# A second MLP in blocks of 512 tokens: first product wider, its weights read again per block

## The chip, the cores and the metric

The kernel runs on one core of a Trainium2 chip. The metric is the device time of one execution in microseconds (us), as the median of several runs.

## The reference

Attention with two kinds of window feeds two MLPs in a row; x is 2304 tokens by 512, both MLPs have 2048 hidden columns. The change touches the second MLP alone:

```python
def _moe2_ref(x, w_in, w_out):
    h = x @ w_in                           # 2304 x 2048
    relu6 = np.clip(h + 3.0, 0.0, 6.0)
    g = h * relu6 / 6.0
    return (g @ w_out).astype(np.float32)  # 2304 x 512
```

## The kernel before, in words

Products are made in three passes of fp32r matmuls (`PASSES`, L624): every operand is split into a high part (a rounded copy, `copy`, L244) and a low part (the rest, `sub`, L247), and high·high, high·low and low·high are summed in PSUM.

**First MLP** (`tile1`, L637): six blocks of 384 tokens, 16 tiles each. A tile is 12 matmuls of the first product (`h`, 384 columns, L629), the activation on ScalarE and VectorE in a buffer of the ring `e` (three buffers; taken by `neg`, L646, free after the split `lo`, L675), and 12 matmuls of the second product (`yp`, L684). The result goes to DRAM as `x2d`.

**Second MLP** (`tile2`, L834): nine blocks `b` of 256 tokens (`N2`), eight tiles `j` each, 72 in all. A tile has two parts.

- The first product `hq`, here called F: two times 12 matmuls of 256 columns (`gemm1`, L626) into one PSUM bank of 512 columns. The weights `w1_i_0`, 16 tiles of 512 KB in the ring `w0`, are loaded once (L792) while the last block of the first MLP frees their buffers, and then stay. One `relu` on ScalarE (L849) and one `mul` on VectorE (L852) over 512 columns make g.
- The second product `m`, here called S: a seven-product (Strassen) scheme, 21 matmuls of 256 columns (L899) in four PSUM banks (`PRODS`, L831). Before it VectorE makes five sums of parts of g (`gf`, L865 to L871), ScalarE rounds (`ga`, `gz`, L245) and VectorE subtracts (`ga`, `gz`, L248). Four of its weight parts stay (`w1_i_1`, L796); the three others, `wx`, 768 KB a tile, stay for even `j` and are read again in each block for odd `j` (L823): 40 loads.

The tokens of a block (`load_x2`, L748) come as four loads of 128 KB from `x2d` (L761) into buffers of the ring `y` (first block) or `e`, then a rounded copy on ScalarE and a subtraction (VectorE or GpSimd in the first block, GpSimd alone later). After the last tile of a block, `y2_out` (L949) adds the seven products up: two copies on ScalarE (L976), eight adds on VectorE (L981), four stores.

The order on every engine is made by a planner (`Plan.run`, L106). Each job has a key (its due time), the engines that can do it with a modelled cost, and what it needs; a ring gives a buffer when its last users have been planned. At each step the job that can start first is taken, the lower key at a tie, and instructions are emitted in that order. On the chip each engine works in that fixed order and waits at each instruction for what it needs. All transfers are issued from SyncE (SP), in order too.

Of the kernel before, what the change touches and what calls it, by code (L numbers as in the profile page):

```python
# [19 lines left out]
P = 128  # L20
# [32 lines left out]
    FULL=("0p0", "0d0", "0d1", "1p0", "1d0", "1d1"),  # L53
    BIAS=0.6,
# [134 lines left out]
def tile_window_attention_two_mlps(  # L189
# [50 lines left out]
    SIZES = dict(w0=KF, w1=KF, raw=3, stg=3, x=4, e=3, y=4, ghl=4, gz=2, wx0=KP // 2, wx1=2, s=2, st=4, a=2, h=2)  # L240
# [22 lines left out]

    SL2 = 5.4

    def at2(b, j):
        return TB[NB1] + SL2 * (b * KP + j)

# [476 lines left out]

    x2, x2_ready, x2_users = {}, {}, {}

    def load_x2(b):  # L748
        key = at2(b - 1, 1) if b else at2(0, 0) - 20
        xu = x2_users[b] = [], []  # L750
        blocks = range(b * N2 // T1, ((b + 1) * N2 - 1) // T1 + 1)
        first = None
        after = tiles2[b - 1, 1][0] if b else tiles[NB1 - 1, 5][0]
        x2_ready[b] = []
        for c in range(KD):
            r, yu = {}, []
            ring = "e" if b else "y"

            def load(e, c=c, r=r):
                r["y"] = take(gp, ring, [P, N2], F32, f"y2_{b}_{c}")  # L760
                nc.sync.dma_start(out=r["y"], in_=x2d[:, c, b * N2:(b + 1) * N2])  # L761

            def hi(e, c=c, r=r):
                if c == 0:
                    x2[b] = [take(xp, "x", [P, 2, 2, N2], F32R, f"x2_{b}_{z}") for z in range(2)]
                copy(e, x2[b][c // 2][:, 0, c % 2], r["y"])

            def lo(e, c=c, r=r):
                z = x2[b][c // 2]
                sub(e, z[:, 1, c % 2], r["y"], z[:, 0, c % 2].bitcast(F32))  # L770

            k = key + c * SL2 * 0.8
            l = job(k, load, {"S": 0.42}, [after, *(x2_done[n, c] for n in blocks)], 0.4, [(RINGS[ring], yu)])
            h = job(
                k + 2, hi, {"A": C["A"](N2)}, [l, first], 0,
                [(RINGS["x"], xu[0]), (RINGS["x"], xu[1])] if c == 0 else (),
            )
            first = first or h
            lj = job(k + 2.1, lo, {"P": C["P"](N2), "D": C["D"](N2)} if not b else {"P": C["P"](N2)}, [h])
            yu += [l, h, lj]  # L780
            xu[c // 2].extend([h, lj])
            x2_ready[b].append(lj)

    def load_w2(i):
        key = at1(NB1 - 1, i) + CFG["LAG"]
        j, k = divmod(i, 2)
        u0 = w_users[1, i, 0] = []
        u1 = w_users[1, i, 1] = []

        def l0(e):  # L790
            w = w_t[1, i, 0] = take(wpool, "w0", [P, 2, DM], F32R, f"w1_{i}_0")
            nc.sync.dma_start(out=w.bitcast(F32), in_=w2d[0][:, i])  # L792

        def l1(e):
# [5 lines left out]
        w2j[i, 0] = job(key, l0, {"S": 0.42}, [last[0], *(w2_done[0, i, c] for c in range(2))], 1.3, [(RINGS["w0"], u0)])  # L800
        w2j[i, 1] = job(key + 0.1, l1, {"S": 0.42}, [last[1], *(w2_done[1, j, 2 * k + c] for c in range(2))], 1.3, [(RINGS["w1"], u1)])
# [3 lines left out]
    def phase(e):  # L805

        p1.close()
        p2["wx"] = ctx.enter_context(tc.tile_pool(name="wx", bufs=KP // 2))
        p2["gt"] = ctx.enter_context(tc.tile_pool(name="gt", bufs=2))

    def load_wx(b, j):

        if j % 2 == 0 and b:
            return wx_j[b - 1, j]
        ring = f"wx{j % 2}"
        u = w_users[2, b, j] = []
        key = at2(b, j) - 11 if b or j % 2 and j > 3 else at1(NB1 - 1, j) + 4

        def load(e):
            if "wx" not in p2:  # L820
                phase(e)
            w = w_t[2, j] = take(p2["wx"], ring, [P, 3, 2, EH], F32R, f"wx{j}_{b}")
            nc.sync.dma_start(out=w.bitcast(F32), in_=w2d[1][:, j, 4:7])  # L823

        return job(key, load, {"S": 0.42}, [*prep_last, *att_users], 2.0, [(RINGS[ring], u)])

    wx_j = {}
    m_tags = deque(["a", "a", "h", "y0", "y1", "y2", "y3"])
# [3 lines left out]
    m_users, tiles2 = {}, {}  # L832

    def tile2(b, j):  # L834


        key = at2(b, j)
        r = {}

        def g1(k):  # L840
            def fn(e):
                if k == 0:
                    r["h"] = ps.tile([P, 2, N2], F32, tag="h", name=f"hq{b}_{j}", bufs=SIZES["h"])
                gemm1(w_t[1, 2 * j + k, 0], x2[b], r["h"][:, k])
            return fn

        def relu(e):
            r["e"] = take(gp, "ghl", [P, 2, N2], F32, f"g{b}_{j}")
            nc.scalar.activation(out=r["e"], in_=r["h"], func=AF.Relu, bias=3.0)  # L849

        def mul(e):
            nc.vector.scalar_tensor_tensor(  # L852
                out=r["e"], in0=r["e"], scalar=6.0, in1=r["h"], op0=ALU.min, op1=ALU.mult
            )


        parts = lambda: r["e"].rearrange("p k (t c) -> p (k t) c", c=P)

        def sums(n):
            def fn(e):  # L860
                if n == 0:
                    r["f"] = take(gp, "ghl", [P, 5, P], F32, f"gf{b}_{j}")
# [18 lines left out]
        def z_hi(e):  # L881
            r["z"] = take(p2["gt"], "gz", [P, 2, 5, P], F32R, f"gz{b}_{j}")
            copy(e, r["z"][:, 0], r["f"])
# [4 lines left out]
        def g2(e):  # L888
            ms = ys.setdefault(("m", b), {})
            for n, bank_ in enumerate(PRODS):  # L890
                if j == 0:
                    y = ps.tile([P, 2, EH], F32, tag=tags[n], name=f"m{b}_{n}", bufs=SIZES.get(tags[n], 1))
                    for z, (k, _, _) in enumerate(bank_):
                        ms[k] = y[:, z]
                for z, (k, ka, kb) in enumerate(bank_):
                    w = w_t[1, 2 * j + kb // 2, 1][:, kb % 2] if kb < 4 else w_t[2, j][:, kb - 4]
                    for s, (a, c) in enumerate(PASSES):
                        g = r["a"][:, a, ka] if ka < 2 else r["z"][:, a, ka - 2]
                        nc.tensor.matmul(  # L899
                            ms[k], g, w[:, c, :], start=(j == 0 and z == 0 and s == 0),  # L900
                            stop=(j == KP - 1 and z == len(bank_) - 1 and s == 2),
                        )

        t = 3 * KD * C["R"](N2)
        hu, eu, fu, au, zu = [], [], [], [], []
        prev = tiles2.get((b, j - 1) if j else (b - 1, KP - 1))
        need = [w2j[2 * j, 0], prev[1] if prev else None]
        if j == 0:
            need += x2_ready[b]
        j1 = job(key, g1(0), {"T": t}, need, 0, [(RINGS["h"], hu)])  # L910
        j2 = job(key + 0.5, g1(1), {"T": t}, [j1, w2j[2 * j + 1, 0]])
        for z in range(2):
            x2_users[b][z].extend([j1, j2])
        w_users[1, 2 * j, 0].append(j1)
        w_users[1, 2 * j + 1, 0].append(j2)
        j3 = job(key + 0.6, relu, {"A": C["A"](2 * N2)}, [j2], 0, [(RINGS["ghl"], eu)])
        j4 = job(key + 0.7, mul, {"D": C["D"](2 * N2)}, [j3])
        j4.sbuf = False
        hu += [j2, j3, j4]
        s = [  # L920
            job(key + 0.8, sums(0), {"D": C["D"](N2)}, [j4], 0, [(RINGS["ghl"], fu)]),
        ]
        s += [job(key + 0.81 + 0.01 * n, sums(n), {"D": C["D"](P if n == 1 else N2)}, [s[0]]) for n in (1, 2)]
        j5 = job(key + 0.9, a_hi, {"A": C["A"](N2)}, [j4], 0, [(RINGS["ghl"], au)])
        j6 = job(key + 0.95, z_hi, {"A": C["A"](5 * P)}, s, 0, [(RINGS["gz"], zu)])
        j7 = job(key + 1.0, a_lo, {"D": C["D"](N2)}, [j5])
        j8 = job(key + 1.1, z_lo, {"D": C["D"](5 * P)}, [j6])
        eu += [j4, *s, j5, j7]
        fu += [*s, j6, j8]
        need = [j7, j8, w2j[2 * j, 1], w2j[2 * j + 1, 1], wx_j[b, j], prev[2] if prev else None]  # L930
        takes = []
        if j == 0:
            tags = []
            m_users[b] = [[] for _ in PRODS]
            for n in range(len(PRODS)):
                tags.append(m_tags[0])
                takes.append((RINGS[m_tags[0]], m_users[b][n]))
                m_tags.rotate(-1)
# [10 lines left out]
    def y2_out(b, key, last):  # L949
# [3 lines left out]
        for u in mu:  # L953
            u.append(last)
# [195 lines left out]
```

## Time and profile before

| | us |
|---|---|
| median of three runs (894.13 to 894.49) | 894.15 |
| profiled execution | 894.27 |
| its span, first to last instruction | 892.3 |

The profiled execution lies 0.12 us above the median, and 1.97 us of it lie outside the span. Times in rows count from the start of the span; mean durations are in ns. PE is TensorE, PEld its weight loads, DVE VectorE, ACT ScalarE, POOL GpSimd, SP the queue of SyncE. A matmul's own duration is longer than the distance to the next one, since they are pipelined: the rate is read from starts.

### The profile page before, as it was taken

How to read it: one execution, taken by the hardware profiler on the slowest of the kernel's cores; microseconds unless marked ns; L12 is line 12 of the kernel's file. 1: busy time of each engine (PE TensorE's matmuls, PEld its weight loads, DVE VectorE, ACT ScalarE, POOL GpSimd, SP SyncE). 2: the span in 40 equal slices, each digit the busy share in tenths (PEclk: the TensorE clock that was granted, in tenths of full speed). 3: DMA queues.
4: the chain of work that ended last, by engine and by line, in shares of the span. 5: the costliest groups of instructions: out<-in, count | busy, mean ns of one | idle time of the engine just before them, and what ended most of it. 6: DMA issues, size and time to landing. Idle time of an engine off the chain costs nothing.

```text
span 892.3 us, 17756 instructions
## 1 busy us (share of the span) xinstructions
PE 865.9 (97%) x6972; PEld 845.0 (95%) x6972; DVE 573.8 (64%) x1244; ACT 428.2 (48%) x1086; POOL 146.0 (16%) x156
## 2 busy tenths in 40 slices
PE   4699999999999999999999999999999999999997
PEld 4599999999999999999999999999999999999997
DVE  6998997878778764543333556565656565756565
ACT  4887865766766763443232333343433343333332
POOL 2655631422323310000000101010101010101000
PEclk9899999999999999999999999999999999999999
DMA  9956548787687862102988523232323232323231
GB/s 347 366 212 245 183 138 276 254 291 250 233 281 266 282 205 86 69 25 78 328 274 255 187 71 119 72 118 72 119 72 119 72 119 72 118 71 119 72 100 54
DMA packets 60627, 149.27 MB, mean 167 GB/s; under 512 B 6272, under 2 KB 28288, under 8 KB 60544
## 3 DMA queue, kind: packets, MB, share of 16 engines
q1 hardware_dynamic: 60544, 148.14, 49.1%
q8 instruction: 55, 0.90, 0.4%
q14 instruction: 28, 0.23, 0.1%
HBM read 115.61 MB, written 32.51 MB: 166 GB/s over the span
## 4 chain that ended last, share of the span: by engine, by line
PE 87%; DVE 5%; DMA 5%; ACT 2%; issue 1%; SPq 0%; POOL 0%; DVEq 0%; ACTq 0%
PE yp L684 21%; PE h L629 21%; PE hq L629 20%; PE m L899 18%; DMA y<-x2d 2%; DVE raw L304 1%; DMA raw<-in_w_in_dram 1%; DMA kTd<-in_kd_dram 1%; DMA w2do<-stg 1%; DVE gz L248 1%; ACT gz L245 0%; DMA vd<-in_vd_dram 0%; DVE gf L871 0%; ACT raw L293 0%; DVE gf L869 0%
## 5 line engine op out<-in xcount | busy, mean ns | idle before, releaser
L629 PE MATMUL hq<-x,w 128*128 128x256 f32 x1728 | 219.2, 283 | 0.0
L684 PE MATMUL yp<-ghl,w 128*128 128x384 f32 x1152 | 218.9, 338 | 0.0
L629 PEld LDWEIGHTS hq<-x,w 128*128 128x128 f32 x1728 | 212.7, 192 | 0.0
L684 PEld LDWEIGHTS yp<-ghl,w 128*128 128x128 f32 x1152 | 199.3, 188 | 1.5
L852 DVE SCALAR_TENSOR_TENSOR g<-g,hq 128x512 f32<-128x512 f32 x72 | 49.4, 686 | 115.5 <-ACT g L849 115.5
L629 PE MATMUL h<-xp,w 128*128 128x384 f32 x576 | 119.3, 341 | 0.0
L629 PE MATMUL h<-xd,w 128*128 128x384 f32 x576 | 115.9, 335 | 1.4 <-DVE xd L561 1.3
L849 ACT ACTIVATE g<-hq 128x512 f32<-128x512 f32 x72 | 43.0, 597 | 144.3 <-PE hq L629 144.1
L648 ACT ACTIVATE e<-h 128x384 f32<-128x384 f32 x96 | 47.2, 492 | 128.6 <-PE h L629 128.3
L629 PEld LDWEIGHTS h<-xd,w 128*128 128x128 f32 x576 | 101.3, 188 | 2.0 <-DVE xd L561 1.5
L629 PEld LDWEIGHTS h<-xp,w 128*128 128x128 f32 x576 | 99.2, 188 | 1.4
L662 DVE SCALAR_TENSOR_TENSOR e<-e,h 128x384 f32<-128x384 f32 x96 | 52.6, 549 | 66.5 <-ACT e L651 66.5
L899 PE MATMUL m<-w,gz 128*128 128x256 f32 x648 | 91.2, 284 | 1.8 <-DVE gz L248 1.7
L248 POOL TENSOR_TENSOR x<-y,x 128x256 fp32r<-128x256 f32 x32 | 25.2, 801 | 401.8 <-ACT x L245 401.8
L899 PEld LDWEIGHTS m<-w,gz 128*128 128x128 f32 x648 | 83.2, 192 | 3.1 <-DVE gz L248 2.7
L248 DVE TENSOR_TENSOR gz<-gf,gz 128x640 fp32r<-128x640 f32 x72 | 59.8, 830 | 35.7 <-ACT gz L245 34.6
L245 ACT CAST gz<-gf 128x640 fp32r<-128x640 f32 x72 | 52.4, 728 | 53.5 <-DVE gf L871 53.5
L899 PE MATMUL m<-wx,gz 128*128 128x256 f32 x432 | 63.6, 283 | 0.0
L248 DVE TENSOR_TENSOR ghl<-e,ghl 128x384 fp32r<-128x384 f32 x90 | 54.5, 606 | 5.5 <-ACT ghl L245 4.1
L899 PEld LDWEIGHTS m<-wx,gz 128*128 128x128 f32 x432 | 57.0, 192 | 0.0
L304 DVE SCALAR_TENSOR_TENSOR raw<-raw 128x512 int32<-128x512 int32 x64 | 51.3, 806 | 5.9 <-ACT raw L293 4.0
L248 POOL TENSOR_TENSOR w<-raw,w 128x512 fp32r<-128x512 f32 x32 | 46.3, 1457 | 35.8 <-DVE w L245 15.6
(438 smaller groups left out, 1044.0 us busy)
## 6 DMA issues: line engine op xcount, KB each, us to landing
wx<-w2do SPq DMA_DIRECT2D x40, 768.0 KB, 4.3
raw<-in_w_in_dram SPq DMA_DIRECT2D x32, 512.0 KB, 6.1
raw<-in_w_out_dram SPq DMA_DIRECT2D x32, 512.0 KB, 6.3
w2do<-stg SPq DMA_DIRECT2D x56, 256.0 KB, 2.5
w2di<-stg SPq DMA_DIRECT2D x32, 256.0 KB, 4.3
w<-w2di SPq DMA_DIRECT2D x16, 512.0 KB, 4.5
w<-w2do SPq DMA_DIRECT2D x16, 512.0 KB, 4.5
qd<-in_qd_dram SPq DMA_DIRECT2D x12, 512.0 KB, 4.4
```

The source lines that it names most:

```text
L245: (nc.scalar.copy if e == "A" else nc.vector.tensor_copy)(out=out, in_=in_)
L248: ENG[e].tensor_tensor(out=out, in0=in0, in1=in1, op=ALU.subtract)
L304: nc.vector.scalar_tensor_tensor(out=hi(), in0=hi(), scalar=3, in1=lo(), op0=ALU.logical_shift_left, op1=ALU.bitwise_or)
L629: nc.tensor.matmul(h, w[:, a, c * P:(c + 1) * P], x[c // 2][:, b, c % 2, :], start=(c == 0 and s == 0), stop=(c == KD - 1 and s == 2),)
L648: nc.scalar.activation(out=r["e"], in_=r["h"], func=AF.Relu, scale=-1.0)
L662: nc.vector.scalar_tensor_tensor(out=r["e"], in0=r["e"], scalar=-1.0, in1=r["h"], op0=ALU.add, op1=ALU.max)
L684: nc.tensor.matmul(ys[b, n], w[:, a, n * P:(n + 1) * P], g[:, c, :], start=(i == 0 and s == 0), stop=(i == KF - 1 and s == 2),)
L849: nc.scalar.activation(out=r["e"], in_=r["h"], func=AF.Relu, bias=3.0)
L852: nc.vector.scalar_tensor_tensor(out=r["e"], in0=r["e"], scalar=6.0, in1=r["h"], op0=ALU.min, op1=ALU.mult)
L899: nc.tensor.matmul(ms[k], g, w[:, c, :], start=(j == 0 and z == 0 and s == 0), stop=(j == KP - 1 and z == len(bank_) - 1 and s == 2),)
```

## The change: what it does

- The first product takes 512 tokens at a time (`N1`): four blocks `c` of 512 and a last one of 256, eight tiles `j` each, 40 in all. A tile is again two times 12 matmuls, now of 512 columns, each dozen in its own PSUM bank (ring `h`, two banks, no longer shared with `m`).
- g is made per half of 256 tokens: `relu` and `mul` over 256 columns, 144 of each instead of 72 over 512. It stays in a new ring `g` of twelve buffers until the second product of that half.
- The second product keeps its 256 tokens. It runs at least `S2` = 5 first-product tiles behind; its sums and splits are due `LEAD2` = 6 us ahead. It is issued in two jobs, of 12 matmuls (banks 0 and 1) and 9 (banks 2 and 3). `gz` moves to the ring `x` (four buffers instead of two), `gf` to a ring of its own (two).
- The ring `w0` now holds the block's tokens (four buffers a block) beside the first product's weights, which are read again for each block: 80 loads of 512 KB instead of 16, each due after the load eight places before it has been used. `wx` is read for every tile: 72 loads instead of 40, in a ring of three, each after the second product three before it.
- All token loads go through the ring `e`, also those of the first block, and their subtractions may go to VectorE or GpSimd.

```diff
-    SIZES = dict(w0=KF, w1=KF, raw=3, stg=3, x=4, e=3, y=4, ghl=4, gz=2, wx0=KP // 2, wx1=2, s=2, st=4, a=2, h=2)
+    SIZES = dict(w0=KF, w1=KF, raw=3, stg=3, x=4, e=3, y=4, ghl=4, wx=3, g=12, f=2, s=2, st=4, a=2, h=2)
...
+    N1 = 2 * N2
+    NB3 = -(-NT // N1)
+    NH = lambda c: min(NT - c * N1, N1) // N2
+    def times2():
+        t = TB[NB1]
+        todo = [(2 * c + h, j) for c in range(NB3) for h in range(NH(c)) for j in range(KP)]
+        for n in range(NB3 * KP):
+            c, j = divmod(n, KP)
+            first2[c, j] = t
+            t += 6 * KD * C["R"](NH(c) * N2)
+            while todo and len(second2) < 2 * (n + 1 - CFG["S2"]) and todo[0][0] // 2 * KP + todo[0][1] < n:
+                second2[todo.pop(0)] = t
+                t += 21 * C["R"](EH)
...
+    def load_x2(c):
+        for k in range(KD):
+            for h in range(NH(c)):
+                key = first2[c - 1, k + 2] + h if c else first2[0, 0] - 20 + 4 * k
+                after = tiles[NB1 - 1, k + 12 * c][0] if c < 2 else tiles2[c - 2, KP - 1]
...
+                    r["y"] = take(gp, "e", [P, N2], F32, f"y2_{c}_{k}_{h}")
...
+                        x2[c, k] = take(wpool, "w0", [P, 2, NH(c) * N2], F32R, f"x2_{c}_{k}")
...
+                after0 = tiles2[c - 1, 0] if c else tiles[NB1 - 1, 3][0]
...
+                lj = job(key + 2.1, lo, {"P": C["P"](N2), "D": C["D"](N2)}, [x])
...
+    def load_w0(c, i):
+        def load(e):
+            w = w_t[3, c, i] = take(wpool, "w0", [P, 2, DM], F32R, f"w1_{c}_{i}_0")
+            nc.sync.dma_start(out=w.bitcast(F32), in_=w2d[0][:, i])
+        n = len(seq2)
+        seq2.append((c, i))
+        last = tiles[NB1 - 1, 4 + n][0] if n < KP else tiles2[seq2[n - KP][0], seq2[n - KP][1] // 2]
+        key = first2[c, i // 2] - 16
...
-        if j % 2 == 0 and b:
-            return wx_j[b - 1, j]
...
+        after = done2[divmod(n - 3, KP)] if n > 2 else start2
+        wx_j[b, j] = job(second2[b, j] - 11, load, {"S": 0.42}, [after, start2], 2.0, [(RINGS["wx"], u)])
...
-    m_tags = deque(["a", "a", "h", "y0", "y1", "y2", "y3"])
+    m_tags = deque(["a", "a", "y0", "y1", "y2", "y3"])
...
+    def gemm2nd(c, j):
+        for k in range(2):
+            def g1(e, r=r, k=k):
+                r["h"] = ps.tile([P, n], F32, tag="h", name=f"hq{c}_{j}_{k}", bufs=SIZES["h"])
+                w = w_t[3, c, 2 * j + k]
+                for d in range(KD):
+                    for s, (a, z) in enumerate(PASSES):
+                        nc.tensor.matmul(r["h"], w[:, a, d * P:(d + 1) * P], x2[c, d][:, z, :],
+                            start=(d == 0 and s == 0), stop=(d == KD - 1 and s == 2))
...
+                def relu(e, r=r, b=b, h=h, k=k):
+                    nc.scalar.activation(out=g_t[b, j][:, k], in_=r["h"][:, h * N2:(h + 1) * N2], func=AF.Relu, bias=3.0)
...
-        j9 = job(key + SL2 + 3.0, g2, {"T": 21 * C["R"](EH)}, need, 0, takes)
+        for n, (banks, size) in enumerate((((0, 1), 12), ((2, 3), 9))):
+            prev = job(
+                key + n * 12 * C["R"](EH), g2(banks), {"T": size * C["R"](EH)}, [*need, prev], 0,
+                [(RINGS[m_tag[b, k]], m_users[b][k]) for k in banks] if j == 0 else (),
+            )
```

## Rows read from the trace of the kernel before

**Rows 1.** The page: busy time by engine; the granted clock in 40 slices.
```profile
PE 865.9 (97%) x6972; PEld 845.0 (95%) x6972; DVE 573.8 (64%) x1244; ACT 428.2 (48%) x1086; POOL 146.0 (16%) x156
...
PEclk9899999999999999999999999999999999999999
```

**Rows 2.** Busy time by stage: the second MLP, and the last 10 us.
```profile
core 0: us, PE busy (x) PEld busy (x) DVE busy (x) ACT busy (x) POOL busy (x), PEclk, DMA share, GB/s
490.70:892.30 401.60, 395.35 (x3266) 393.58 (x3264) 236.74 (x507) 141.72 (x269) 25.16 (x32) 1.00 0.31 97
881.90:892.30 10.40, 5.60 (x43) 5.00 (x41) 5.55 (x14) 2.39 (x5) 0.00 (x0) 0.95 0.15 51
```

**Rows 3.** Timeline, TensorE: starts of S (its first three matmuls) in the second MLP.
```profile
500.75 0.52 PE L899 MATMUL m<-wx,ga 128*128 128x256 f32 x3
...
593.21 0.52 PE L899 MATMUL m<-wx,ga 128*128 128x256 f32 x3
599.21 0.52 PE L899 MATMUL m<-wx,ga 128*128 128x256 f32 x3
...
881.80 0.52 PE L899 MATMUL m<-wx,ga 128*128 128x256 f32 x3
```

**Rows 4.** The chain that ended last, 584 to 600 us: start us, us, what.
```profile
586.49 5.49 DMA y<-x2d
...
593.48 1.15 DVE gz L248
...
594.67 1.82 PE m L899 x13
596.49 2.88 PE hq L629 x24
```

**Rows 5.** Waits, 490 to 892 us: us in total, times, longest us.
```profile
ACT x L245 <- DMA y<-x2d: 13.0, 10, 2.8
```

**Rows 6.** Timeline, TensorE and the first stores, at the end.
```profile
885.99 1.10 PE L899 MATMUL m<-w,gz 128*128 128x256 f32 x7 [0.31 <-DVE gz L248]
...
886.93 0.88 PE L899 MATMUL m<-wx,gz 128*128 128x256 f32 x6
```

**Rows 7.** Timeline, TensorE, around the end of the first MLP.
```profile
480.45 2.24 PE L684 MATMUL yp<-ghl,w 128*128 128x384 f32 x12
482.53 1.20 PE L629 MATMUL h<-xp,w 128*128 128x384 f32 x6
...
490.85 1.59 PE L629 MATMUL hq<-x,w 128*128 128x256 f32 x12
```

**Rows 8.** Groups by line and shape, 570 to 880 us: busy us, mean ns.
```profile
L852 DVE SCALAR_TENSOR_TENSOR g<-g,hq 128x512 f32<-128x512 f32 x57 | 39.1, 686 | 89.2 <-ACT g L849 89.2
...
L849 ACT ACTIVATE g<-hq 128x512 f32<-128x512 f32 x57 | 34.0, 597 | 113.4 <-PE hq L629 113.2
...
L981 DVE SCALAR_TENSOR_TENSOR o<-m,o 128x256 f32<-128x256 f32 x56 | 20.3, 415 | 0.0
...
L976 ACT ACTIVATE o<-m 128x256 f32<-128x256 f32 x14 | 4.6, 381 | 0.9
```

**Rows 9.** The page, DMA issues: KB each, median us from issue to landing.
```profile
wx<-w2do SPq DMA_DIRECT2D x40, 768.0 KB, 4.3
...
w<-w2di SPq DMA_DIRECT2D x16, 512.0 KB, 4.5
...
y<-x2d SPq DMA_DIRECT2D x36, 128.0 KB, 4.3
```

**Rows 10.** Busy time by stage (columns as in rows 2): the last block of the first MLP.
```profile
426.00:460.00 34.00, 34.00 (x199) 34.00 (x197) 12.79 (x27) 11.55 (x26) 0.00 (x0) 1.00 0.90 305
460.00:495.00 35.00, 35.00 (x209) 35.00 (x209) 11.79 (x24) 8.01 (x16) 0.00 (x0) 1.00 0.79 252
```

**Rows 11.** Timeline: an activation of the first MLP, first and last use of `e`.
```profile
439.05 0.49 ACT L648 ACTIVATE e<-h 128x384 f32<-128x384 f32 x1 [3.11 <-PE h L629]
...
441.19 0.56 DVE L248 TENSOR_TENSOR ghl<-e,ghl 128x384 fp32r<-128x384 f32 x1
```

More of the change, by code (lines that the diff above doesn't have):

```diff
@@ L743, in tile_window_attention_two_mlps @@
     tiles, y_users, wj = {}, {}, {}
-    x2, x2_ready, x2_users = {}, {}, {}
[L748 to L782, printed above, removed]
@@ new lines, in load_w0 @@
+    def load_w0(c, i):
+        u = w_users[3, c, i] = []
+        def load(e):
[5 more added lines that the diff above has]
+        key = first2[c, i // 2] - 16
+        w2j[c, i, 0] = job(key, load, {"S": 0.42}, [last, *(w2_done[0, i, z] for z in range(2))], 1.3, [(RINGS["w0"], u)])
@@ L785, in load_w2, with load_w1, load @@
+    def load_w1(i):
         key = at1(NB1 - 1, i) + CFG["LAG"]
         j, k = divmod(i, 2)
[L787 to L794, printed above, removed]
+        u = w_users[1, i, 1] = []
+        def load(e):
             w = w_t[1, i, 1] = take(wpool, "w1", [P, 2, 2, EH], F32R, f"w1_{i}_1")
@@ L827, in tile_window_attention_two_mlps, with mul @@
+        wx_j[b, j] = job(second2[b, j] - 11, load, {"S": 0.42}, [after, start2], 2.0, [(RINGS["wx"], u)])
     wx_j = {}
-    m_tags = deque(["a", "a", "h", "y0", "y1", "y2", "y3"])
+    m_tags = deque(["a", "a", "y0", "y1", "y2", "y3"])
     PRODS = (((3, 1, 4), (2, 0, 3)), ((4, 4, 1), (0, 2, 2)), ((1, 3, 0), (5, 5, 6)), ((6, 6, 5),))
-    m_users, tiles2 = {}, {}
+    m_users, tiles2, done2, split2 = {}, {}, {}, {}
+    g_t, g_done, g_users = {}, {}, {}
+    m_tag = {}
+    def gemm2nd(c, j):
+        key = first2[c, j]
+        nh = NH(c)
+        n = nh * N2
+        prev = tiles2.get((c, j - 1) if j else (c - 1, KP - 1))
+        for h in range(nh):
+            g_users[2 * c + h, j] = []
+            g_done[2 * c + h, j] = []
+        new = {}
+        for k in range(2):
+            r = {}
+            def g1(e, r=r, k=k):
[3 more added lines that the diff above has]
+                    for s, (a, z) in enumerate(PASSES):
+                        nc.tensor.matmul(
+                            r["h"], w[:, a, d * P:(d + 1) * P], x2[c, d][:, z, :],
+                            start=(d == 0 and s == 0), stop=(d == KD - 1 and s == 2),
+                        )
+            hu = []
+            t = 3 * KD * C["R"](n)
+            j1 = job(key + k * t, g1, {"T": t}, [w2j[c, 2 * j + k, 0], prev, *(x2_ready[c] if j == 0 and k == 0 else ())], 0, [(RINGS["h"], hu)])
+            hu.append(j1)
+            w_users[3, c, 2 * j + k].append(j1)
+            prev = tiles2[c, j] = j1
+            for d in range(KD):
+                x2_users[c, d].append(j1)
+            for h in range(nh):
+                b = 2 * c + h
+                def relu(e, r=r, b=b, h=h, k=k):
+                    if k == 0:
+                        g_t[b, j] = take(p2["g"], "g", [P, 2, N2], F32, f"g{b}_{j}")
+                    nc.scalar.activation(
+                        out=g_t[b, j][:, k], in_=r["h"][:, h * N2:(h + 1) * N2], func=AF.Relu, bias=3.0
+                    )
+                def mul(e, r=r, b=b, h=h, k=k):
+                    nc.vector.scalar_tensor_tensor(
+                        out=g_t[b, j][:, k], in0=g_t[b, j][:, k], scalar=6.0, in1=r["h"][:, h * N2:(h + 1) * N2],
+                        op0=ALU.min, op1=ALU.mult,
+                    )
+                q = key + t * (k + 1) + 0.1 * h
+                j3 = job(q, relu, {"A": C["A"](N2)}, [j1, start2, new.get(b)], 0, [(RINGS["g"], g_users[b, j])] if k == 0 else ())
+                new.setdefault(b, j3)
+                j4 = job(q + 0.1, mul, {"D": C["D"](N2)}, [j3])
+                j4.sbuf = False
+                hu += [j3, j4]
+                g_users[b, j] += [j3, j4]
+                g_done[b, j].append(j4)
@@ L834, in tile2 @@
     def tile2(b, j):
-        key = at2(b, j)
+        key = second2[b, j]
+        lead = key - CFG["LEAD2"]
         r = {}
[L840 to L857, printed above, removed]
+        parts = lambda: g_t[b, j].rearrange("p k (t c) -> p (k t) c", c=P)
         def sums(n):
@@ L886, in z_lo @@
             sub(e, r["z"][:, 1], r["f"], r["z"][:, 0].bitcast(F32))
[L888 to L902, printed above, removed]
@@ L915, in tile2 @@
[L915 to L924, printed above, removed]
@@ L925, in tile2, with g2, fn @@
[L925 to L933, printed above, removed]
+        def g2(banks):
+            def fn(e):
+                ms = ys.setdefault(("m", b), {})
+                for n in banks:
+                    if j == 0:
+                        tag = m_tag[b, n]
+                        y = ps.tile([P, 2, EH], F32, tag=tag, name=f"m{b}_{n}", bufs=SIZES.get(tag, 1))
+                        for z, (k, _, _) in enumerate(PRODS[n]):
+                            ms[k] = y[:, z]
+                    for z, (k, ka, kb) in enumerate(PRODS[n]):
+                        w = w_t[1, 2 * j + kb // 2, 1][:, kb % 2] if kb < 4 else w_t[2, b, j][:, kb - 4]
+                        for s, (a, c) in enumerate(PASSES):
+                            g = r["a"][:, a, ka] if ka < 2 else r["z"][:, a, ka - 2]
+                            nc.tensor.matmul(
+                                ms[k], g, w[:, c, :], start=(j == 0 and z == 0 and s == 0),
+                                stop=(j == KP - 1 and z == len(PRODS[n]) - 1 and s == 2),
+                            )
+            return fn
@@ L952, in y2_out @@
         bank_of = {k: n for n, bank_ in enumerate(PRODS) for k, _, _ in bank_}
-        for u in mu:
-            u.append(last)
+        for n, u in enumerate(mu):
+            u.append(last[n // 2])
         chain = {}
```

113 lines of the change are left out of this document (72 added, 41 removed).

## The prediction

> **What bounds the kernel now.** I read the page first [rows 1]: TensorE is busy 97% of the span at a granted clock of nine tenths or more in all but one of 40 slices, VectorE 64%. Then the stage that the change touches [rows 2]: in the second MLP TensorE works 395.35 of 401.60 us at clock 1.00, while VectorE has 59%, ScalarE 35% and the transfers 97 GB/s. So TensorE sets the time here, and only two things can shorten the stage: fewer TensorE cycles, or less of its idle time.
>
> The idle time is small and has two places. One tile is F, 2.88 us [rows 4], and S, 21 matmuls of 0.12 us, 2.52 us: 5.40 us. From the first S to the 71st, 70 intervals, this would be 378.0 us; the starts lie 881.80 - 500.75 = 381.05 us apart [rows 3], so 3.05 us are lost on the way. The pattern is the interval of 6.00 us after 593.21, 0.60 too long; the other losses of this size sit at changes of block too. The chain tells why [rows 4]: a load of tokens lands 5.49 us after its issue, ScalarE, which works in order, waits for it, the splits behind it come late, and S waits for `gz`. In the whole stage ScalarE waits so 13.0 us in ten waits, the longest 2.8 [rows 5]. The second place is the end: the last S could follow the one at 881.80 directly, its last six matmuls would then start at 881.80 + 5.04 - 0.72 = 886.12, and they start at 886.93 [rows 6], 0.81 late, because the last tile's splits follow its own F.
>
> **The change, part by part.**
>
> *Wider matmuls.* 384 columns take (482.53 - 480.45)/12 = 173.3 ns from start to start [rows 7]; 256 columns take 2.88/24 = 120.0 ns [rows 4]. The difference, 53.3 ns for 128 columns, is 0.4167 ns a column, and 13.3 ns are left over at both widths. No row shows 512 columns; by the same line they take 226.7 ns, and two of 256 take 240.0. Four of the five blocks are wide: 4 x 8 x 24 = 768 matmuls, each 13.3 ns cheaper than the pair it replaces: **-10.24 us**. The last block (192 matmuls of 256) and all of S stay. Bounds: nothing (512 columns cost twice 256) to 10.24; I take the line, since two widths lie on it. The Trainium skill, "TensorE: Matmul & The Clock Gate", section "Back-to-back issue gap", gives a gap of columns/2.4 GHz plus about 2.5 ns; by it the fixed part saved would be 768 x 2.5 ns, about 1.9 us in place of 10.2. These rows disagree with it at 256 and 384 columns.
>
> *Idle at changes of block.* S now uses a g made at least five tiles before, with splits due 6 us ahead and buffers for up to four S. A late load may still hold ScalarE for 2.8 us or, with fuller queues, longer, but that delay no longer goes straight to S. Of 3.05 us I take **-2.5**; bounds 0 and 3.05. What is late next would be the release of `h`, below.
>
> *The end.* The last F is followed by four S, so the last splits have 7.6 us and more: **-0.8** (0 to 0.81). The adds and stores after the last S are as before.
>
> *g in halves.* 72 `relu` of 597 ns become 144 of about 381, and 72 `mul` of 686 ns become 144 of about 415 (the same shapes out of PSUM) [rows 8]: ScalarE +11.9 us, VectorE +10.4, that is 40% and 64% of some 388 us. Hidden by TensorE: **0**. Where the cover is thin is the start: five tiles of F alone, a dozen of 2.72 us each, on two banks. A bank is free about 2 x 0.381 + 0.415 = 1.2 us after its last matmul, which leaves 1.5 us. The next block's eight token loads fall in this stretch; a ScalarE wait of 1.3 us (13.0/10) fits, the longest would cost 1.3, eight of them 10. I take **+0.5**.
>
> *The first tokens through `e`.* An activation of the first MLP holds a buffer from 439.05 to 441.75 [rows 11] in every 4.16 us (24 x 173.3 ns). A token load holds one about 4.3 us for landing [rows 9] and 1 us for the split. Twelve tiles before the end, 50 us, three buffers offer 150 us; eight loads and twelve activations ask for 42 + 32. **0**, at most 5.3 once, if all three are held when an activation wants one; the second product runs some tiles behind and covers most of that.
>
> *Weights streamed.* This adds 64 loads of 512 KB and 32 of 768 KB. A wide tile with its two S takes 5.44 + 5.04 = 10.48 us and asks for two loads of each kind, 2.62 MB, and 0.26 MB of tokens and stores: 275 GB/s in place of 97. The nearest row is the last block of the first MLP, which streams such loads [rows 10]: 305 GB/s over 34 us with TensorE busy 34.00 of 34.00, at a DMA share of 0.90. A `wx` load is freed by the S three before it, so it has 2.52 + 5.44 + 2.52 = 10.48 us (the worse of each pair) against 4.3 to land [rows 9]. SP issues in order: a load queued behind the stores of a block waits for eight adds of 0.415 us [rows 8], 3.3 us, and still has 2.9 left. So **0** in the wide blocks. In the last block a tile with two S takes 7.92 us, and in its first four tiles the demand is (2.62 + 0.13)/7.92 = 348 GB/s. At 305 GB/s that is 9.0 us a tile, +4.4 us over four; at 305/0.90 = 339 it is 8.1, +0.8; the time in hand may hide it all. I take **+1.2** (0 to 4.4). The four S at the end follow each other, so a load has 5.04 us; with the 5.49 of [rows 4] and the issue it would come 0.8 late. I take **+0.3** (0 to 0.8).
>
> **Sum**, against the profiled execution: 894.27 - 10.24 - 2.5 - 0.8 + 0.5 + 1.2 + 0.3 = 882.7, or **882.6** on the scale of the median, which lies 0.12 below it. With every gain whole and no cost it is 880.0; nothing else of TensorE's idle time is touched.
>
> **Rivals.**
>
> *Eaten in part.* Loads land later under the new traffic: ScalarE's waits grow, F waits for `h` at the start, S for `wx` in the last block. With no gain from idle time, 4 us at the start and 4.4 in the last block it is 894.15 - 10.24 + 8.4 = 892.3; the case covers 886 to 892.3. For it: ScalarE already waits [rows 5]. Against: every wait has more time in hand than before.
>
> *Slower: the transfers become the bound.* Place: `wx` loads from the first S on. After the eight loads made ahead the stage moves 72 loads of 512 KB, 72 of 768 KB and 64 of 128 KB, 102.8 MB. TensorE's part now lasts from 490.85 [rows 7] to 886.93 + 6 x 0.12 = 887.65 [rows 6], 396.8 us: below 259 GB/s the new stage is longer than the old. At the 252 GB/s of the second part of [rows 10] it lasts 408 us, +11.2: 905. For it: that row streams these very weights and reaches no more. Against: its share is only 0.79, TensorE was never idle there, each load waited for its buffer to come free, and the row before it has 305. The Trainium skill, "DMA: Bandwidth & Descriptors", section "Bandwidth", asks for 1 MiB and more in a transfer for three quarters of the peak, and by its fit (2.0 us plus bytes at 436 GB/s) the four loads of a tile one after the other would take about 14 us. The rows show them overlapping.
>
> *Not what it says: no cheaper columns.* If 512 columns cost 240 ns, the first term is gone: 882.6 + 10.2 = 892.8. No row of 512 columns excludes it; the two widths on one line speak against it. The rule quoted above on the gap is this case, softened: 890.9.
>
> **How the numbers follow.** About 0.2%, 1.8 us, is what a measurement of this kernel can tell from no change: faster means below 892.4, slower above 895.9. Forecast, 880 to 886: 0.66. Eaten in part: 0.17, of which 0.01 ends within 0.2%. Transfers as bound, or another stall of more than 13 us: 0.12. No cheaper columns: 0.05. So faster 0.82, same 0.06, slower 0.12. The range takes the forecast and the first rival, from the floor to its dearest end: 880.0 to 892.3, which leaves out about 0.17.
>
> **What would show it.** Right: 960 `hq` matmuls, the wide ones 226.7 ns apart; the stage's TensorE work shorter by 10 us; no gap of 0.6 us at changes of block; the last S without a wait; some 265 GB/s over the stage at a DMA share under 0.9, with no TensorE wait on `wx`. Wrong: TensorE waiting for `wx` or for first-product weights all through the wide blocks (transfers); waits for `relu` or `mul` before F (bank `h`), or gaps before S in the last block (eaten in part); 240 ns between wide matmuls (no cheaper columns); or idle time in the last block of the first MLP, where there is none now (ring `e`).

## The result and the profile after

The changed kernel takes 884.71 us in the median of four runs (883.75 to 885.75), the kernel before 894.14 us beside it: ratio 0.9898, 95% interval 0.988 to 0.9916. That is 9.4 us less where 11.5 were forecast, inside the range of 880.0 to 892.3. The profiled execution of the changed kernel took 885.54 us, 8.7 less than the one of before.

First the page of the changed kernel, the lines that answer to [rows 1] and [rows 9]; the last two are DMA issues with KB each and the median time to landing.

```profile
PE 855.8 (97%) x6204; PEld 804.3 (91%) x6204; DVE 573.1 (65%) x1335; ACT 427.8 (48%) x1158; POOL 130.6 (15%) x137
...
wx<-w2do SPq DMA_DIRECT2D x72, 768.0 KB, 4.7
w<-w2di SPq DMA_DIRECT2D x80, 512.0 KB, 5.3
```

TensorE issues 768 matmuls fewer and still sets the time. The weight loads are busy 40.7 us less, the matmuls 10.1. The loads from DRAM land a little later than before, 4.7 and 5.3 us in place of 4.3 and 4.5.

Busy time by stage (columns as in [rows 2]): two pieces of the wide blocks; a piece with their last 16 us and the first 16 us of the last block, whose F starts at 794.02; then the second half of this piece alone.

```profile
610.00:694.00 84.00, 84.00 (x529) 76.12 (x528) 52.58 (x132) 31.22 (x76) 3.04 (x4) 1.00 0.78 274
694.00:778.00 84.00, 84.00 (x528) 76.14 (x527) 51.02 (x130) 29.63 (x72) 1.53 (x2) 1.00 0.77 269
778.00:810.00 32.00, 32.00 (x245) 30.93 (x244) 20.50 (x55) 11.71 (x28) 0.00 (x0) 1.00 0.92 330
794.00:810.00 16.00, 16.00 (x136) 16.00 (x135) 8.19 (x21) 5.40 (x12) 0.00 (x0) 1.00 1.00 379
```

The demand of 275 GB/s is there (274, 269), then 379 GB/s as the last block begins, and TensorE is busy throughout. VectorE is at 61 to 64% in the first three rows.

Waits of the second MLP, to set beside [rows 5] (us in total, times, longest us):

```profile
ACT x L247 <- DMA y<-x2d: 9.8, 8, 1.9
...
PE m L968 <- DMA wx<-w2do: 3.3, 3, 1.6
```

ScalarE still waits for token loads, but nothing on TensorE follows from it. Instead TensorE waits for `wx`, three times. The timeline of TensorE shows where: after the last first product.

```profile
835.78 1.60 PE L879 MATMUL hq<-x,w 128*128 128x256 f32 x12
837.22 0.52 PE L968 MATMUL m<-wx,ga 128*128 128x256 f32 x3
...
854.86 0.52 PE L968 MATMUL m<-wx,ga 128*128 128x256 f32 x3
...
857.38 0.52 PE L968 MATMUL m<-wx,ga 128*128 128x256 f32 x3
...
860.91 0.62 PE L968 MATMUL m<-wx,ga 128*128 128x256 f32 x3 [0.85 <-DMA wx<-w2do]
...
865.23 0.59 PE L968 MATMUL m<-wx,ga 128*128 128x256 f32 x3 [1.55 <-DMA wx<-w2do]
...
870.34 0.52 PE L968 MATMUL m<-wx,ga 128*128 128x256 f32 x3
...
873.92 0.59 PE L968 MATMUL m<-wx,ga 128*128 128x256 f32 x3 [0.91 <-DMA wx<-w2do]
...
876.51 0.52 PE L968 MATMUL m<-wx,ga 128*128 128x256 f32 x3
```

The first line is the last dozen of F, each of the others the start of an S. Fifteen follow the last F, 2.52 us apart as long as nothing is late: 857.38 to 860.91 is 1.01 too long, the next 1.80, 870.34 to 873.92 is 1.06 (and the first S after a wait takes up to 0.07 more). From first to last they are 39.29 us apart, fourteen times 2.52 would be 35.28: **4.0 us are lost here**.

The chain that ended last gives the loads behind the second and the third of these waits (start us, us, what), and SP's timeline what it did before the load of 858.61:

```profile
858.24 0.27 SPq L257
...
858.61 6.49 DMA wx<-w2do
...
868.01 5.78 DMA wx<-w2do
```

```profile
855.20 0.34 SPq L257 DMA_DIRECT2D out_dram<-o  x1
855.63 0.38 SPq L847 DMA_DIRECT2D wx<-w2do  x1
856.19 2.32 SPq L257 DMA_DIRECT2D out_dram<-o  x3
858.61 5.42 SPq L847 DMA_DIRECT2D wx<-w2do  x3
```

The buffer of the load at 858.61 was free when the S begun at 854.86 ended, at 857.38; SP stood at the three stores, which waited for VectorE. The load then took 6.49 us. The one at 868.01 was held by nothing and took 5.78, where the two S in between leave 5.04 (its lead: from the free buffer to the S that needs the load).

How long the loads of `wx` take among these fifteen S depends on what else is under way. Issued from 839 to 854 us, one every 2.52 us; then from 855.5 to 872, with and after the four stores:

```profile
DMA to landing us min/median/max: 4.1/4.2/4.2
```

```profile
DMA to landing us min/median/max: 5.1/5.5/6.9
```

A lead of 5.04 us is enough for the first group and too short for the second.

Why fifteen and not four? The timeline of a wide block shows the order:

```profile
507.33 2.91 PE L879 MATMUL hq<-x,w 128*128 128x512 f32 x12
510.07 0.52 PE L968 MATMUL m<-w,gz 128*128 128x256 f32 x3
510.43 0.88 PE L968 MATMUL m<-wx,gz 128*128 128x256 f32 x6
511.15 2.91 PE L879 MATMUL hq<-x,w 128*128 128x512 f32 x12
513.89 0.52 PE L968 MATMUL m<-wx,ga 128*128 128x256 f32 x3
```

A dozen of F, the second part of an S, a dozen of F, the first part of an S: one S for a tile of F, though a tile makes g for two. The planner counts what follows a TensorE job as ready 0.25 us after it (`enter`, L115), on TensorE itself too. The second dozen of a tile or the second part of an S can never start at once in its reckoning, so it takes the other chain each time. S falls behind until the twelve buffers of g are full, and the last block, with F of 256 columns, goes on in the same way; the arrears are worked off at the end.

The same timeline prices a wide dozen: 513.89 - 511.15 = 2.74 us, where 2.72 was reckoned.

**One way to compare traces.** The start of the second MLP lies between 490.3 and 492.8 us in the traces below, since what comes before it differs between executions; so I compare the stage: from the start of the first F to the end of the last S (the start of its last matmul and 0.12 us). Each row is one trace. "Lost at the end" is what the S after the last F are late, start to start against 2.52 us.

| kernel | stage, us | S after the last F | lost at the end | stage without it |
|---|---|---|---|---|
| before | 396.80 | | | |
| before, token loads counted at 2.8 (early) | 393.73 | | | |
| changed | 388.35 | 15 | 4.01 | 384.34 |
| changed, second trace (again) | 386.70 | 15 | 2.24 | 384.46 |
| two of 256 for each 512 (narrow) | 395.47 | 15 | 2.42 | 393.05 |
| paired order (pairs) | 383.40 | 4 | 0 | 383.40 |
| four `wx`, nine g (ring4) | 386.10 | 11 | 0 | 386.10 |
| three `wx`, nine g (g9) | 388.75 | 11 | 3.15 | 385.60 |
| stores on GpSimd's queue (stores) | 385.33 | 15 | 1.07 | 384.26 |
| stores after the loads (late) | 387.31 | 15 | 2.91 | 384.40 |
| paired, one copy more a tile (extra1) | 383.40 | 4 | 0 | 383.40 |
| paired, two copies more a tile (extra2) | 383.41 | 4 | 0 | 383.41 |

### The profile page after: what moved, and what is told of

It is laid out like the page before. It is cut to its first block, busy times and chain, and to the rows that moved or that the text cites. A ratio compares the mean times of both kernels' runs of the same rounds, so it can differ in the third digit from the quotient of the medians.

```text
span 883.7 us, 16684 instructions
## 1 busy us (share of the span) xinstructions
PE 855.8 (97%) x6204; PEld 804.3 (91%) x6204; DVE 573.1 (65%) x1335; ACT 427.8 (48%) x1158; POOL 130.6 (15%) x137
## 4 chain that ended last, share of the span: by engine, by line
PE 92%; DVE 3%; DMA 3%; ACT 1%; issue 1%; SPq 0%; POOL 0%; DVEq 0%; ACTq 0%; POOLq 0%
PE hq L879 23%; PE yp L681 22%; PE h L626 22%; PE m L968 18%; DMA wx<-w2do 1%; DMA raw<-in_w_in_dram 1%; DVE raw L301 1%; DMA kTd<-in_kd_dram 1%; DVE o L1042 0%; DVE xd L558 0%; PE ps0d L472 0%; ACT raw L290 0%; DVE w L247 0%; ACT ptd L247 0%; DVE raw L298 0%
## 5 line engine op out<-in xcount | busy, mean ns | idle before, releaser
L879 PE MATMUL hq<-x,w 128*128 128x512 f32 (+1 forms) x960 | 211.9, 370 | 0.0
L879 PEld LDWEIGHTS hq<-x,w 128*128 128x128 f32 x960 | 164.6, 189 | 26.6
L898 ACT ACTIVATE g<-hq 128x256 f32<-128x256 f32 x144 | 50.3, 382 | 144.2 <-PE hq L879 117.7
L903 DVE SCALAR_TENSOR_TENSOR g<-g,hq 128x256 f32<-128x256 f32 x144 | 56.3, 417 | 74.8 <-ACT g L898 72.8
L968 PE MATMUL m<-w,gz 128*128 128x256 f32 x648 | 95.5, 283 | 0.0
L968 PEld LDWEIGHTS m<-w,gz 128*128 128x128 f32 x648 | 87.4, 192 | 2.3
L250 POOL TENSOR_TENSOR x<-y,x 128x256 fp32r<-128x256 f32 x13 | 9.7, 749 | 332.3 <-ACT x L247 332.3
```

The source lines that it names most:

```text
L250: ENG[e].tensor_tensor(out=out, in0=in0, in1=in1, op=ALU.subtract)
L879: nc.tensor.matmul(r["h"], w[:, a, d * P:(d + 1) * P], x2[c, d][:, z, :], start=(d == 0 and s == 0), stop=(d == KD - 1 and s == 2),)
L898: nc.scalar.activation(out=g_t[b, j][:, k], in_=r["h"][:, h * N2:(h + 1) * N2], func=AF.Relu, bias=3.0)
L903: nc.vector.scalar_tensor_tensor(out=g_t[b, j][:, k], in0=g_t[b, j][:, k], scalar=6.0, in1=r["h"][:, h * N2:(h + 1) * N2], op0=ALU.min, op ...
L968: nc.tensor.matmul(ms[k], g, w[:, c, :], start=(j == 0 and z == 0 and s == 0), stop=(j == KP - 1 and z == len(PRODS[n]) - 1 and s == 2),)
```

## The experiments

**The width alone.** Each matmul of 512 columns becomes two of 256; the planner's costs, and so the order, stay.

```diff
-                for d in range(KD):
-                    for s, (a, z) in enumerate(PASSES):
-                        nc.tensor.matmul(
-                            r["h"], w[:, a, d * P:(d + 1) * P], x2[c, d][:, z, :],
...
+                for q in range(nh):
+                    cols = slice(q * N2, (q + 1) * N2)
+                    for d in range(KD):
+                        for s, (a, z) in enumerate(PASSES):
+                            nc.tensor.matmul(
+                                r["h"][:, cols], w[:, a, d * P:(d + 1) * P], x2[c, d][:, z, cols],
...
```

> Each wide matmul of 512 columns is issued as two of 256 into the same bank; order, loads and all else stay. If the width brings the gain (a dozen of 512 takes 2.745 us in the trace of the changed kernel, two dozens of 256 take 2.88): 64 dozens x 0.135 = 8.6 us more than the changed kernel, about 893.3 us, 0.999 of the kernel before; TensorE's waits for wx at the end remain, about 4 us. If 13.3 ns a matmul is the full price as predicted: 10.2 us more, 894.9. If the gain came from order and leads instead: less than 3 us more, below 888.

Measured: 893.98 us, ratio 0.9996 (0.9986 to 1.0006). Its timeline at the same place:

```profile
507.53 3.04 PE L881 MATMUL hq<-x,w 128*128 128x256 f32 x24
510.41 0.52 PE L970 MATMUL m<-w,gz 128*128 128x256 f32 x3
```

24 matmuls take 2.88 us where twelve wide ones took 2.74. Without the end the stage is 393.05 - 384.34 = 8.7 us longer, the 8.6 of the first theory and not 10.2. Everything else in the change, the streamed weights, the order, the kept g, comes out within the measurement of nothing. In this trace it wins 3.9 us between blocks and in the last splits and loses 2.4 at the end, a stage 1.3 us shorter than before; the medians show no difference, and where the other executions lose the rest no trace shows.

**The order on TensorE.** What follows a TensorE job on TensorE counts as ready at once.

```diff
-            j1 = job(key + k * t, g1, {"T": t}, [w2j[c, 2 * j + k, 0], prev, *(x2_ready[c] if j == 0 and k == 0 else ())], 0, [(RINGS["h"], hu)])
+            j1 = job(key + k * t, g1, {"T": t}, [w2j[c, 2 * j + k, 0], (prev, -0.25) if prev else None, *(x2_ready[c] if j == 0 and k == 0 else ())], 0, [(RINGS["h"], hu)])
...
-                key + n * 12 * C["R"](EH), g2(banks), {"T": size * C["R"](EH)}, [*need, prev], 0,
+                key + n * 12 * C["R"](EH), g2(banks), {"T": size * C["R"](EH)}, [*need, (prev, -0.25) if prev else None], 0,
```

> Only the planner's order changes: what follows a TensorE job on TensorE itself counts as ready at once, not 0.25 us later, so that a whole first-product tile is followed by two whole second products, and four second products are left after the last first product, not fifteen. Theory (the run of fifteen outpaces a ring of three loads): the waits for wx, 4.0 us, are gone, and with half as many handovers from a 512-column dozen to the second product (20 ns each) another 0.6: 880 to 881 us, 0.985 of the kernel before. Rival (the transfers are too slow in the last block as such, 348 GB/s asked): waits for wx of 2 to 4 us appear between the first products of the last block: 883 to 885. Rival (the release of h binds when both dozens follow each other): TensorE waits for relu or mul before first products, 0.3 us and more a tile, 885 or above.

Measured: 881.51 us, ratio 0.9863 (0.9849 to 0.9876), an interval that lies below that of the change itself (0.988 to 0.9916); all four times (880.71 to 882.26) lie below all eight of the changed kernel that were taken here (the lowest is 883.75): faster than both kernels. Its timeline in a wide block and at the end:

```profile
534.01 5.63 PE L879 MATMUL hq<-x,w 128*128 128x512 f32 x24
539.48 0.52 PE L968 MATMUL m<-wx,ga 128*128 128x256 f32 x3
...
862.45 3.04 PE L879 MATMUL hq<-x,w 128*128 128x256 f32 x24
865.33 0.52 PE L968 MATMUL m<-wx,ga 128*128 128x256 f32 x3
...
867.85 0.52 PE L968 MATMUL m<-wx,ga 128*128 128x256 f32 x3
...
870.37 0.52 PE L968 MATMUL m<-wx,ga 128*128 128x256 f32 x3
...
872.89 0.52 PE L968 MATMUL m<-wx,ga 128*128 128x256 f32 x3
```

A whole tile of F (5.47 us), then two S, and four S at the end without a gap: the picture that the prediction had drawn. TensorE waits for nothing in the whole stage; neither the last block nor the release of `h` costs anything, so both rivals fall. In this order the first four tiles of the last block ask for what the prediction reckoned, 348 GB/s, and get it:

```profile
807.00:839.00 32.00, 32.00 (x269) 32.00 (x268) 22.21 (x58) 12.05 (x27) 0.00 (x0) 1.00 0.97 348
```

Of the four S at the end only the last has a load with a lead of 5.04 us, issued at 868.05, and that lands in 4.1 us; the two loads before it were issued while F still lay between. The stage is 0.9 us below that of the change without its end: some 0.6 are half as many changes of width (29 runs of wide matmuls in place of 63), the rest two short waits for the bank `h`, 0.13 us each, that the changed kernel has at 637.46 and 721.76.

**A longer ring for `wx`, and its control.**

```diff
-    SIZES = dict(w0=KF, w1=KF, raw=3, stg=3, x=4, e=3, y=4, ghl=4, wx=3, g=12, f=2, s=2, st=4, a=2, h=2)
+    SIZES = dict(w0=KF, w1=KF, raw=3, stg=3, x=4, e=3, y=4, ghl=4, wx=4, g=9, f=2, s=2, st=4, a=2, h=2)
...
-        after = done2[divmod(n - 3, KP)] if n > 2 else start2
+        after = done2[divmod(n - 4, KP)] if n > 3 else start2
```

The control has `wx=3, g=9` and `n - 3`.

> Four buffers for wx in place of three, paid for with nine buffers of g in place of twelve (eleven second products follow each other at the end). Theory (lead too short): a load then has 3 x 2.52 = 7.56 us against 5 to 6.5 to land: no wait for wx, 4 us less than the changed kernel, about 880.7. Rival (768 KB every 2.52 us, 312 GB/s, is more than the transfers deliver over such a run): waits shrink to no less than half, 882.5 or more. Rival (nine buffers of g hold first products back): waits of first products for g, slower than 884.7.

> Control for the run before: nine buffers of g, wx still three. Theory (lead too short): eleven second products in a row in place of fifteen, still more than three loads can feed: waits for wx of 2 to 4 us stay, 883 to 885 us. If g was what mattered: as fast as with four buffers of wx.

Measured: with four buffers 882.86 us, 0.9878 (0.9865 to 0.9892); with three 886.25, 0.9915 (0.990 to 0.993). TensorE's waits for `wx` are gone in the trace with four; in the control they stay, as its timeline shows:

```profile
864.77 0.63 PE L968 MATMUL m<-wx,ga 128*128 128x256 f32 x3 [1.14 <-DMA wx<-w2do]
867.76 0.59 PE L968 MATMUL m<-wx,ga 128*128 128x256 f32 x3 [0.21 <-DMA wx<-w2do]
873.22 0.59 PE L968 MATMUL m<-wx,ga 128*128 128x256 f32 x3 [0.19 <-DMA wx<-w2do]
876.46 0.59 PE L968 MATMUL m<-wx,ga 128*128 128x256 f32 x3 [0.50 <-DMA wx<-w2do]
```

So eleven S in a row, one every 2.52 us, can be fed when a load has 7.56 us and not when it has 5.04: the time to landing is what lacks, not the rate. (In both, the stores of the last block but one fall among them, and single loads take 6.4 to 7.0 us.) The time came out above the 880.7 expected: first products start late in six places in the wide blocks, 0.24 us in five and 0.78 in one, and the stage is 1.8 us longer than that of the change without its end. That the smaller ring of g does this is argued from the control, where six such places stand too, 0.24 to 0.25 us each. What F waits for there is not g but the release of its bank `h`: each time it starts 0.10 us after the `mul` that frees the bank. In five places this `mul` stands behind the eight adds of `y2_out` in VectorE's order, as here in the trace with four buffers; F starts at 615.19:

```profile
612.03 2.74 DVE L1042 SCALAR_TENSOR_TENSOR o<-m,o 128x256 f32<-128x256 f32 x8
614.68 0.74 DVE L903 SCALAR_TENSOR_TENSOR g<-g,hq 128x256 f32<-128x256 f32 x2
```

In the sixth, the 0.78, the `relu` before it stands behind two token copies on ScalarE, the first of which waited 1.27 us for its load. So the rival held in part, by another way than it named, and a late token load can still reach TensorE through `h`.

**The idle time between blocks, in the kernel before.** One number in the planner:

```diff
-            l = job(k, load, {"S": 0.42}, [after, *(x2_done[n, c] for n in blocks)], 0.4, [(RINGS[ring], yu)])
+            l = job(k, load, {"S": 0.42}, [after, *(x2_done[n, c] for n in blocks)], 2.8 if b else 0.4, [(RINGS[ring], yu)])
```

> The kernel before, with one number changed: the planner counts 2.8 us in place of 0.4 for a token load of the second MLP (after the first block), so that ScalarE's copies of it are placed later in its order, behind splits that do not need them. Theory (late token loads hold ScalarE, and the splits behind it): the 3.05 us of idle time at changes of block go, the 0.8 at the end stays: about 891.1 us, 0.9965 of the kernel before. Rival (the eight adds of y2_out on VectorE hold the splits there): no change, 894.

Measured: 891.22 us, ratio 0.9962 (0.9948 to 0.9976). ScalarE's waits for token loads, 13.0 us in [rows 5], are not in its trace any more, every S but the last starts 5.40 us after the one before, and of TensorE's waits in the stage one line is left, that of the end:

```profile
PE m L899 <- DVE gz L248: 0.3, 1, 0.3
```

The stage takes 393.73 us, 3.07 less than before, as the theory said (3.05). The adds of `y2_out` are where they were, so the rival falls.

**SP's order at the end.** Two edits to the changed kernel; in the first the stores go through GpSimd's queue, in the second the stores of the last block but one come after the last load of `wx`.

```diff
-            d = dma(key + 0.01 * n, lambda: out[r0:r0 + P, c0:c0 + EH], lambda: o[rc], [chain[rc]], us=0.4)
+            d = job(key + 0.01 * n, lambda e: nc.gpsimd.dma_start(out=out[r0:r0 + P, c0:c0 + EH], in_=o[rc]), {"S": 0.42}, [chain[rc]], 0.4)
```

```diff
+    held = []
...
+            if b == NB2 - 2:
+                held.append(d)
...
+        for d in held:
+            d.need.append((wx_j[NB2 - 1, KP - 1], -2.0))
         plan.run()
```

> The changed kernel with the stores of the result issued from GpSimd's queue instead of SP's; order and all else as they are. Theory (mostly lead: three loads of 5 us cannot feed a second product every 2.52 us): the first two waits for wx shrink by what SP was held by the three stores, 1.2 us in all, the last wait (1.06) stays: 883.5. Rival (SP's order alone): waits for wx under 0.5 us in all, 880.7. Rival (SP's order is of no matter): 884.7.

> The changed kernel once more, beside the next run. Theory: waits for wx among the fifteen second products at the end, about 4 us, and 0.99 of the kernel before. Rival (the waits of the first trace were chance): under 1 us of them.

> The changed kernel with the four stores of the last block but one issued after the last load of wx instead of between the loads; TensorE's order is the same. Theory (SP's order starts the waits, a lead of 5.04 us keeps them): the first two waits (1.01 and 1.80 us) shrink to under 1 us together, the last (1.06) stays or shrinks: 2 to 3 us less than the run beside it, about 0.987 of the kernel before. Rival (only the lead counts): waits for wx as before, 3 us and more. Rival (only SP's order counts): no wait for wx, 4 us less, 0.9855.

Measured: `stores` 886.14 us, 0.9902 (0.9882 to 0.9922); the changed kernel again 884.97, 0.9893 (0.9873 to 0.9913); `late` 882.40, 0.9864 (0.9845 to 0.9882). The second trace of the unchanged order lost 2.24 us at the end where the first lost 4.01: the loads landed in 5.47 and 5.53 us on its chain, not 6.49 and 5.78. This scatter is as large as what the two edits could show in one trace each; besides, the trace of `stores` is of its fastest execution (883.73) and that of `late` of its slowest (884.12). In `late` the two waits lie elsewhere; its chain:

```profile
849.64 5.61 DMA wx<-w2do
855.26 0.14 issue
855.39 12.84 PE m L969 x105
868.23 0.02 issue
868.25 6.66 DMA wx<-w2do
```

Between them every S starts on time, also where SP had stood at the stores: the four loads issued from 857 to 866 us land as fast as undisturbed ones.

```profile
DMA to landing us min/median/max: 4.2/4.3/4.5
```

The last load shares the engines with the held stores that follow it at 868.62 and takes 6.66 us. So neither edit takes the waits away. A lead of 5.04 us is enough for a load with nothing beside it (4.1 to 4.5 us) and too short for one that lands in 5.5 to 6.7; the stores make some of the loads that late, and moving them moves the wait. They are not all of it: the loads at 849.64 here and at 868.01 in the changed kernel (5.61 and 5.78 us) have no store near them. Beside each of these two the trace has one packet of 16 KB on the queue that the profile calls "instruction" (q8); other loads with such a packet beside them landed in 4.1 to 4.3 us, and whether it holds a load up no run shows. What SP's order adds to the time is left open: `late` is some 2.5 us below the run beside it, but the intervals touch, and `stores` shows fewer waits in its trace and no gain in its time. Part of that may be the queue: from the end of the last S to the end of the span it takes 5.8 us (875.78 to 881.6), with SP's stores 4.7 in the changed kernel (879.03 to 883.7) and 4.6 to 5.0 in all other traces.

**How near the transfers are to binding.** The paired kernel, with copies that nobody waits for, in the second to fourth block, one or two a tile:

```diff
+    dup = dram.tile([P, KF, 2, DM], F32, name="dup")
...
+        def again(e):
+            nc.sync.dma_start(out=dup[:, i], in_=w2d[0][:, i])
+
+        if 0 < c < 4 and i % 2 >= 1:
+            job(key + 0.01, again, {"S": 0.0}, [w2j[c, i, 0], start2])
```

(`>= 0` for two a tile.)

> The kernel with paired order (880 to 882 us), with one more copy of 512 KB for each tile of the second to fourth block (24 in all), between two places in DRAM, issued from SP behind the weights and waited for by nobody: 275 GB/s asked become 325 over 24 x 10.48 = 252 us. Theory (the transfers have room, 305 to 340 GB/s): 0 to 16 us longer, and at 340 no wait for wx but at the fourth block. Rival (275 GB/s is already what they can give): 252 x 0.18 = 46 us longer.

> The same with two more copies a tile: 375 GB/s asked. Theory (room to 340): 252 x 0.10 = 26 us longer, with TensorE waiting for wx and first-product weights; with room to 305 only, 58 us. Rival (room far above 340): no longer than 5 us.

Measured, one execution each: 880.84 and 880.60 us. Busy time from 576 to 828 us (columns as in [rows 2]), of the paired kernel, with one copy and with two:

```profile
576.00:828.00 252.00, 252.00 (x1629) 230.91 (x1628) 154.51 (x392) 90.93 (x218) 10.50 (x13) 1.00 0.86 278
```

```profile
576.00:828.00 252.00, 252.00 (x1633) 231.16 (x1632) 154.16 (x392) 90.32 (x218) 10.90 (x14) 1.00 0.92 318
```

```profile
576.00:828.00 252.00, 252.00 (x1634) 231.18 (x1633) 154.91 (x395) 91.53 (x221) 11.27 (x14) 1.00 0.97 361
...
wx<-w2do SPq DMA_DIRECT2D x50, 768.0 KB, 6.5
```

361 GB/s at a DMA share of 0.97, and TensorE still works every microsecond; the stage is 383.41 us, as without the copies. A `wx` load lands in 6.5 us instead of 4.3, which its 10.48 us hide. The estimate of 305 to 340 GB/s that the prediction had read off [rows 10] was too low: that row showed what was asked there, not what could be given. (About a fifth of the 361 are the copies, which go from DRAM to DRAM; the 348 and 379 GB/s above have none.)

## Why the prediction was right, and where its terms were off

The mechanism held: TensorE sets the stage's time before and after, and the gain is its own. By the terms, in the profiled execution (stage 396.80 to 388.35, -8.45):

- *Wider matmuls*, forecast -10.24: **-8.6**. Within a run of wide matmuls the line holds: from the sixth of a dozen on the starts lie 226.7 ns apart, as reckoned. What the two widths could not show is the change of width. After matmuls of 256 columns the first five starts of a dozen of 512 lie 233, 236, 228, 233 and 231 ns apart (medians of 62 dozens in the trace of the change); back at 256 columns the first two lie 114 and 119 apart in place of 120. That is 21 ns net for each of 63 runs of wide matmuls, 1.3 us; the two short waits for `h` named under the paired order add 0.3. 10.24 - 1.3 - 0.3 = 8.6, and the run with the width alone undone gives 8.7. The prediction's sentence on the Trainium skill, "TensorE: Matmul & The Clock Gate", "Back-to-back issue gap", took only the gap of an isolated matmul, about 2.5 ns over columns/2.4 GHz, which gives an estimate of 215.8 ns at 512 columns; for a stream with its weight loads the same section has about 131 ns. The trace has 226.7 and decides against both.
- *Idle at changes of block*, forecast -2.5: **-3.05**, all of it. That late token loads made it is shown in the kernel before by one number of the planner. ScalarE's waits are still there, 9.8 us, and reach nothing.
- *The end's splits*, forecast -0.8: **-0.8**.
- *Start*, +0.5, and *last block*, +1.2: **0** both. At the start no F waited for `h`; in the whole stage it came late twice, by 0.13 us. In the last block 379 GB/s were delivered over its first 16 us, and 348 over its first four tiles in the paired order.
- *The four S at the end*, +0.3 with 0.8 as bound: **+4.0** (2.2 in a second trace). This is the step that failed: the number of S was wrong, and with it what falls among them. With four, as the paired order has them, one load has a lead of only 5.04 us, it lands in 4.1 and nothing is lost. With fifteen, twelve loads have it; the stores of the block before come among them, the last six loads take 5.1 to 6.9 us, and three S wait. I took four S from the due times and did not follow the planner's rule of readiness, which [rows 7] could have suggested: there, too, dozens of the two products of the first MLP alternate strictly.

-8.6 - 3.05 - 0.8 + 4.0 = -8.45. Against the stage of this execution the forecast was 3.1 us too good: the wide matmuls and the end cost 1.6 and 3.7 us more than reckoned, the idle time between blocks and the two feared costs that did not come gave 2.2 back. On the medians it was 2.1; the second trace loses less at the end (2.24), the other executions have no trace. So it is partly luck that the time came this near: errors of 5.3 and 2.2 us went opposite ways.

Of the rivals, "eaten in part" named the place (S waiting for `wx` late in the stage) with another cause. "Transfers as the bound" was far from deciding: 361 GB/s are not enough to bring it about in the paired order. "No cheaper columns" fell with the first wide dozen. In the prediction's sentence on the Trainium skill, "DMA: Bandwidth & Descriptors", the fit stands in that page's section "Anatomy of one DMA — SWDGE (gpsimd) path" and, like the table behind the advice of 1 MiB, for transfers issued from GpSimd; the loads here go from SP, and 348 GB/s, mostly of loads of 512 and 768 KB that take 4 us and more each, show them overlapping. The ring `e` cost nothing: TensorE is busy without a break through the last block of the first MLP.

## What to carry to other kernels

A lookahead is a time, not a count of buffers: three loads ahead were 10.5 us while other work lay between the consumers and 5 us once it was used up, so ask what the last stretch of a stage looks like, in which order its consumers really stand, and what else is on the queues then (a load took 4.2 us alone and up to 6.9 beside and after four stores). An order planned by "what can start first" follows its latencies: an allowance of 0.25 us made for a semaphore, applied to an engine's own next job, put fifteen consumers in a row. And a transfer rate read from a row is a demand, not a limit, as long as the engine that it feeds is never idle.

## What the runs showed of the hardware that was not expected

- A change of width costs time in the first matmuls of 512 columns: after some of 256 columns their starts lie 233, 236, 228, 233 and 231 ns apart before they settle at 226.7, and back at 256 columns the first two lie 114 and 119 ns apart in place of 120: 21 ns net for each change to 512 and back (63 in the trace of the change). From F to S at 256 columns nothing of the kind is seen (71 places in the kernel before, 120 ns).
- 361 GB/s over 252 us, about a fifth of it copies from DRAM to DRAM, left TensorE's rate as it was, to 0.01 us in 383.4; the landing of a 768 KB load went from 4.3 to 6.5 us.
- Loads of 768 KB, one every 2.52 us, landed in 4.1 to 4.2 us with nothing else under way, and in 5.1 to 6.9 with and after four stores of 128 KB.
- Stores issued from GpSimd's queue ended about 1 us later after the last matmul than those from SP's (5.8 us in one trace against 4.6 to 5.0 in eleven).
